# A spectral mixer with two expert layers on one core: new planner offsets, input in quarters, last spreads, gates and stores rearranged

## The chip, the core and the metric

The kernel runs on one core of a Trainium2 chip. The core has TensorE (PE in the rows; PEld is its weight load), VectorE (DVE), ScalarE (ACT), GpSimd (POOL) and SyncE (SP), each with its own instruction stream, and 16 DMA engines that serve the queues of SP, ACT and POOL. The metric is the device time of one execution in microseconds: 1768.54 us for the kernel before, the median of 3 runs (1767.31 to 1769.47).

## What is computed

The reference has three parts, each in float32, on 8 sequences of 3072 rows with 256 columns:

```
X = rfft(x, axis=1)                      # over the 3072 rows
Yr, Yi = complex product of X with (w_r, w_i), plus biases
y = irfft(soft_shrink(Yr) + i soft_shrink(Yi))

logits = y @ phi                         # 24576 rows, 8 experts x 4 slots
d = softmax over the rows;  slot_in = d.T @ y
slot_out = relu(slot_in @ w1) @ w2       # per expert, F = 1024
z = softmax over the slots of logits @ slot_out

out = (silu(z @ w_gate) * (z @ w_val)) @ w_out   # width 1536
```

The three moe2 weights come as float64, and the kernel makes float32 of them itself.

## The kernel before, in words

**First half (phase1, up to about 655 us).** The eight sequences are batches b = 0 to 7. Each goes through: stage_a (sixteen units; in each a matmul of 16 columns of x with a transform table into a PSUM bank, mm, and a transpose of that bank by VectorE into the tile chan, turn; there are two such banks), stage_c (the second step of the transform, in three blocks g = 0 to 2, with ScalarE, VectorE and GpSimd splitting its output in two parts), stage_b (the product with w_r and w_i, six products per block), after_b (bias and shrink, into the tile yt), stage_q (product with phi, and the transposes turn_y of yt), and the spreads: DMAs that carry yt to the tile yi with partitions and blocks exchanged, sixteen of 64 KB for each block. When the three blocks of a batch are done, logits, slots and combine follow. In logits, sp_out (L1031, ScalarE) fills one column of vpad, turn (L1017, VectorE) transposes vpad, and l_mm, colmax, keep_l, newmax, lower and expo come after one another. In slots, slot_mm (L1242) multiplies with the spread tile yi; its last two groups need the third block's. combine makes the scores over the slots and stores them to c_scr in DRAM. Beside these, narrow makes float32 of the float64 weights, and mix_w, part_w and rest_w prepare w_r and w_i once at the beginning.

**The order.** Every step is handed to a planner (class Plan) by add(engine, duration, rank, function, reads, writes, ...). The planner then emits the instructions one by one: among the tasks whose inputs are planned, it takes the one that can start first by its own times (COST and the durations given), and among those that can start together the one of lowest rank. A rank is a place in the batch sequence plus an offset from SHIFT, found by the task's name; a prime in the name is for the last batch, and a triple has one offset for each block. A name that is not in SHIFT has the offset 0. Engines execute in the order in which they were given their instructions. So SHIFT decides order and nothing else.

**The start.** load_f loads the table of stage_a, load_first (L681) the first batch in two halves of 128 columns, put the tables of stage_c (cm) and others, load_w (L1402) w_r, w_i and the biases by four DMAs; all are issued by SP.

**The end of the first half.** The third block of batch 7 is spread in four parts (yi_parts, L913) of four DMAs, all from SP. free_x, free_a and free_b close pools when their last readers are planned, and the expert weights (w1 and w2, sixteen loads of 1 MB by POOL's queue) go to the freed space. hold adds 80 small matmuls that write to a bank nobody reads.

**Second half (after_slots).** The 32 slots go through w1 and w2, then gates(t) (L1673) multiplies the result with a third of w_gate and w_val (t = 0, 1, 2, 512 columns each) and writes gstk. The main loop has 576 steps: gv(i) makes pg and pv of a block of 128 inner columns from gstk and the scores cst, split(i - 1) makes a high and a low part of silu(pg) * pv, and mm_out(i - 3) adds six products to the output banks; inner block f = i mod 12 needs the gate group t = f // 4. After each twelfth step two transposes and four DMAs store 512 rows' worth of output (L1732). The schedule of the loop is written out:

```
        for i in range(n + 3):
            for t in {0: (0, 1), 6: (2,)}.get(i, ()):
                gates(t)
            if i < n:
                gv(i)
            if 1 <= i <= n:
                split(i - 1)
            if i >= 3:
                mm_out(i - 3)
```

Of the kernel before, what the change touches and what calls it, by code (L numbers as in the profile page):

```python
# [10 lines left out]
F32 = mybir.dt.float32  # L11
# [11 lines left out]
R1 = 96  # L23
R2 = 32
# [135 lines left out]
for _n, _w in (  # L160
# [14 lines left out]


SHIFT = {
    "stage_a.mm": -9.84,
    "stage_a.turn": 0.54,
    "stage_c.mm": (-9.05, -7.24, -16.09),  # L180
    "stage_c.hi": (24.47, -33.15, -38.97),
    "stage_c.lo": (14.18, 18.71, -22.9),
    "stage_c.one_part": (-18.23, 22.67, -8.15),
    "stage_c.add_part": (-13.36, 13.63, -10.4),
    "stage_c.sum_hi": (14.45, 11.1, -10.23),
    "stage_c.sum_lo": (17.84, -9.25, -3.5),
    "stage_c.last_mm": (-1.22, 0.0, 0.0),
    "stage_c.last_out": (2.01, 0.0, 0.0),
    "stage_b.last_mm": (-3.14, 0.0, 0.0),
    "stage_b.last_out": (-37.61, 0.0, 0.0),  # L190
    "stage_b.mm": (-0.54, -0.28, -0.45),
    "after_b.take": (43.36, -0.88, 16.29),
    "after_b.gather": (-2.04, -56.11, 7.1),
    "after_b.relu": (29.62, 5.9, 11.56),
    "after_b.join": (8.77, 14.98, -9.65),
    "stage_q.mm": (0.04, -3.83, 3.24),
    "stage_q.turn_y": (-1.8, 21.9, 7.71),
    "stage_q.turn": (-17.81, 21.29, -10.62),
    "stage_q.spread": (9.56, -31.65, 30.86),
    "logits.inv_mm": -0.29,  # L200
    "logits.sp_mm": -20.44,
    "logits.sp_out": 3.1,
    "logits.rot": 25.23,
    "logits.join": -8.39,
    "logits.turn": -19.78,
    "logits.l_mm": 20.77,
    "logits.colmax": -10.52,
    "logits.keep_l": 6.71,
    "logits.spread": -20.81,
    "logits.max_mm": -6.92,  # L210
    "logits.newmax": 40.03,
    "logits.factor": 6.44,
    "logits.bc_mm": -20.03,
    "logits.lower": -9.17,
    "logits.expo": -9.83,
    "slots.f_mm": -1.07,
    "slots.turn": 7.27,
    "slots.cross": -13.47,
    "slots.rot": 1.28,
    "slots.join": -7.11,  # L220
    "slots.d_mm": -3.64,
    "slots.evac": -12.82,
    "slots.slot_mm": -9.92,
    "slots.gather": -15.51,
    "combine.rowmax": 14.19,
    "combine.lower": -34.43,
    "combine.expo": -29.05,
    "combine.total": 8.18,
    "combine.scale": -28.91,
    "combine.turn": -24.49,  # L230
    "combine.hi": 6.73,
    "combine.lo": 11.01,
    "combine.store": -13.51,
    "narrow.load": 18.5,
    "narrow.bits": -4.56,
    "narrow.size": 21.96,
    "narrow.value": -10.54,
    "narrow.store": 8.48,
    "load_x": 17.41,
    "narrow.part": 15.19,  # L240
    "narrow.rest": -35.44,
    "stage_q.mm'": (0.0, 0.0, -24.61),
    "stage_q.turn_y'": (0.0, 0.0, 7.19),
    "stage_q.turn'": (0.0, 0.0, 4.21),
    "stage_q.spread'": (0.0, 0.0, -25.35),
    "logits.inv_mm'": -24.89,
    "logits.sp_mm'": -13.07,
    "logits.sp_out'": 30.05,
    "logits.rot'": 3.97,
    "logits.join'": 15.9,  # L250
    "logits.turn'": -2.34,
    "logits.l_mm'": -42.59,
    "logits.colmax'": 37.25,
    "logits.keep_l'": 19.77,
    "logits.spread'": 15.02,
    "logits.max_mm'": -13.41,
    "logits.newmax'": -7.99,
    "logits.factor'": 24.36,
    "logits.bc_mm'": 12.34,
    "logits.lower'": -12.24,  # L260
    "logits.expo'": 34.68,
    "slots.f_mm'": 31.04,
    "slots.turn'": 17.34,
    "slots.cross'": 4.58,
    "slots.rot'": 0.07,
    "slots.join'": 40.67,
    "slots.d_mm'": 14.24,
    "slots.evac'": -15.02,
    "slots.slot_mm'": -41.69,
    "slots.gather'": -2.53,  # L270
    "combine.rowmax'": 29.49,
    "combine.lower'": -3.91,
    "combine.expo'": 1.28,
    "combine.total'": 25.68,
    "combine.scale'": 43.19,
    "combine.turn'": 51.36,
    "combine.hi'": -1.63,
    "combine.lo'": 2.88,
    "combine.store'": 10.46,
    "fetch_w1": -9.92,  # L280
    "fetch_w2": 8.18,
    "fetch_wg": 4.29,
}


# [208 lines left out]
def kernel(  # L494
# [79 lines left out]
    def phase1():  # L574
# [103 lines left out]
        add("DVE", 3.0, -9, setup_small, w=["small", "vpad", "M"])  # L678


        def load_first(dh):  # L681
            def go():
                T["x0", dh] = t = early.tile([R1, R2, 128], F32, name=f"x0{dh}")
                nc.sync.dma_start(
                    out=t, in_=x[0, :, dh * 128:(dh + 1) * 128].rearrange("(p n) d -> p n d", n=R2)
                )

            return go
# [15 lines left out]
        def stage_a(b, p, rank):  # L704
            dq, dd = divmod(p, 4)
            dh, d0 = dq // 2, (dq % 2) * 64 + dd * 16
            kq = ("xq", b, dq) if b else ("x0", dh)
            kt, ka = ("tt", b, dh), ("ac", "a", b, p)
            d1 = dd * 16 if b else d0

            def mm():
                pt = bank(ka, [128, R2, 16], "ac")
                nc.tensor.matmul(  # L713
                    out=pt, lhsT=fwd[:, 8 - 8 * dh:136 - 8 * dh], rhs=T[kq][:, :, d1:d1 + 16], start=True, stop=True
                )

            def turn():
                nc.vector.transpose(  # L718
                    out=chan[:, 12 * dh:12 * dh + 16, d0:d0 + 16, :].rearrange("p j d i -> p d j i"),
                    in_=T[ka].rearrange("p n d -> p d n"),  # L720
                )
# [192 lines left out]
            return [[e] for e in range(4)] if (b, g) == (B - 1, 2) else [list(range(4))]  # L914

        def yi_keys(b, g):
            return [("yi", b, g, part[0]) for part in yi_parts(b, g)]

        def stage_q(b, g, rank):

# [24 lines left out]

                return go

            def spread(part):
                def go():
                    if part[0] == 0:  # L950
                        sb(ypool, ki, [128, 2, 4, 2, 4, 32], "yi", 4)
                    for e in part:
                        for q in range(4):
                            nc.sync.dma_start(
                                out=T[ki][32 * q:32 * q + 32, :, e].rearrange("p h c s k -> p h (c s k)"),
                                in_=T[ky][32 * e:32 * e + 32, :, q].rearrange("p h c f -> p h (c f)"),
                            )
# [7 lines left out]
            add("DVE", 0.33, rank, turn, r=[(*kp, 0)], w=[(*kq, g)], new=("qt", kq) if g == 0 else None)  # L965
            for part in yi_parts(b, g):
                add(
                    "SP", 0.25 * len(part), rank, spread(part), r=[(*ky, eh, co) for eh in range(2) for co in range(2)],
                    w=[(*ki, part[0])], new=("yi", ki) if part[0] == 0 else None, bus=0.74 * len(part), dmas=4 * len(part),
                )  # L970

        def times(eng, out, v, tw):
            e = nc.vector if eng == "DVE" else nc.gpsimd
# [457 lines left out]
        for b in range(B):  # L1431
            t0 = 3 * b
            a0, a1 = t0 - 1.6, t0 - 0.45
            da = (a1 - a0) / 16
            for dh in range(2 * (b == 0)):
                add("SP", 0.06, -9 + dh, load_first(dh), w=[("x0", dh)], bus=4.37)
            for dq in range(4):
                if b == 0 and dq == 3:
                    constants(0)
# [95 lines left out]
        for t in (0, 1):  # L1535
            add(
                "SP", 0.12, TT + 0.9, fetch_wg(t), w=[("wg", t)], bus=2.91, dmas=2, new=("yt", ("wg", t)),
                after=[("ws", i) for i, (_, d) in enumerate(jobs) if len(d) == 1] + [("yi", last, 2, 0), ("w2", E - 2), "w2x"],
            )
        def hold(i):  # L1540

# [17 lines left out]
    def after_slots(ypool):  # L1559
# [150 lines left out]
        def mm_out(i):  # L1710
# [12 lines left out]
            if f == NF - 1:  # L1723

                for k in range(2):
                    nc.vector.transpose(
                        out=ob_t[0][:, :, k, :], in_=po_t[0][k].rearrange("p (n l) -> p n l", l=32)
                    )
                r0 = b * SEQ + q * 1024
                to = out[r0:r0 + 1024].rearrange("(l n) (c e) -> c l n e", n=32, c=4)  # L1730
                for c in range(4):
                    nc.sync.dma_start(  # L1732
                        out=to[c, :, 16 * rh:16 * rh + 16],
                        in_=ob_t[0][32 * c:32 * c + 32].rearrange("p n h o -> p n (h o)"),
                    )

        n = len(steps)
        for i in range(n + 3):
            for t in {0: (0, 1), 6: (2,)}.get(i, ()):
                gates(t)  # L1740
            if i < n:
                gv(i)
# [41 lines left out]
```

## Time and profile before

| | us |
|---|---|
| median of 3 runs | 1768.54 (1767.31 to 1769.47) |
| the profiled execution | 1769.84 |
| its span, first to last instruction | 1768.0 |
| TensorE busy in the span | 1704.9 |
| VectorE, ScalarE, GpSimd busy | 1276.0, 981.8, 307.8 |
| SP's DMA queue | 103.59 MB, 29.1% of the 16 DMA engines' time |
| POOL's DMA queue | 29.36 MB, 6.9% |

A row of a timeline has the start in us from the span's first instruction, the duration, the engine (SPq: the queue that SP issues to; the duration is that of the issuing), the line, the operation, the tiles written and read, how many instructions were merged into the row, and in brackets the idle time before it with what ended that. A matmul on float32 data is two records.

### The profile page before, as it was taken

How to read it: one execution, taken by the hardware profiler on the slowest of the kernel's cores; microseconds unless marked ns; L12 is line 12 of the kernel's file. 1: busy time of each engine (PE TensorE's matmuls, PEld its weight loads, DVE VectorE, ACT ScalarE, POOL GpSimd, SP SyncE). 2: the span in 40 equal slices, each digit the busy share in tenths (PEclk: the TensorE clock that was granted, in tenths of full speed). 3: DMA queues.
4: the chain of work that ended last, by engine and by line, in shares of the span. 5: the costliest groups of instructions: out<-in, count | busy, mean ns of one | idle time of the engine just before them, and what ended most of it. 6: DMA issues, size and time to landing. Idle time of an engine off the chain costs nothing.

```text
span 1768.0 us, 23212 instructions
## 1 busy us (share of the span) xinstructions
PE 1704.9 (96%) x8266; PEld 1292.7 (73%) x8266; DVE 1276.0 (72%) x2116; ACT 981.8 (56%) x1809; POOL 307.8 (17%) x292
## 2 busy tenths in 40 slices
PE   6999999999998989999999999999999999999998
PEld 3666565666665665888888888888888888888886
DVE  4678878787786544777777777777777777777776
ACT  1565545546563514556655566556665566655664
POOL 1335345445454641000000000000000000000000
PEclk9999999999999989999999999999999999999999
DMA  9456564564774497112112112113112113111111
GB/s 183 72 120 126 132 139 88 132 134 100 146 159 143 147 326 149 24 25 51 25 24 52 24 25 51 25 24 51 24 25 51 25 24 52 24 25 24 24 23 26
DMA packets 252292, 134.44 MB, mean 76 GB/s; under 512 B 196912, under 2 KB 237584, under 8 KB 252176
## 3 DMA queue, kind: packets, MB, share of 16 engines
q1 hardware_dynamic: 241968, 103.59, 29.1%
q0 software_dynamic: 10208, 29.36, 6.9%
q8 instruction: 65, 1.06, 0.3%
q14 instruction: 51, 0.42, 0.1%
HBM read 69.99 MB, written 37.75 MB: 61 GB/s over the span
## 4 chain that ended last, share of the span: by engine, by line
PE 89%; DVE 5%; ACT 2%; DMA 1%; issue 1%; SPq 1%; POOL 0%; DVEq 0%; ACTq 0%; POOLq 0%
PE o L1719 45%; PE pb L830 9%; PE pg L1694 8%; PE pv L1695 8%; PE ac L713 6%; PE ac L735 4%; PE ch L928 1%; PE pb L1545 1%; PE ch L1242 1%; PE ch L1054 1%; PE ch L1190 1%; PE ch L988 1%; PE ch L1146 1%; PE pg L1678 1%; SPq L673 0%
## 5 line engine op out<-in xcount | busy, mean ns | idle before, releaser
L1719 PE MATMUL o<-hh,wo 128*128 128x512 f32 x2304 | 723.0, 395 | 0.0
L1699 DVE TENSOR_TENSOR h<-sg,pv 128x512 f32<-128x512 f32 x576 | 394.4, 685 | 271.5 <-ACT sg L1697 270.1
L1697 ACT ACTIVATE sg<-pg 128x512 f32<-128x512 f32 x576 | 344.4, 598 | 421.7 <-PE pg L1694 421.7
L1719 PEld LDWEIGHTS o<-hh,wo 128*128 128x128 f32 x2304 | 434.6, 189 | 100.4
L1719 PE MATMUL o<-hl,wo 128*128 128x512 f32 x1152 | 454.1, 394 | 0.0
L1707 DVE TENSOR_TENSOR hl<-h,hh 128x512 fp32r<-128x512 f32 x576 | 393.6, 683 | 0.2
L1706 ACT ACTIVATE hh<-h 128x512 fp32r<-128x512 f32 x576 | 359.6, 624 | 0.7 <-DVE h L1699 0.7
L1719 PEld LDWEIGHTS o<-hl,wo 128*128 128x128 f32 x1152 | 216.4, 188 | 51.6 <-DVE hl L1707 0.2
L1694 PE MATMUL pg<-cst,gstk 96*128 96x512 f32 x576 | 228.2, 396 | 0.0
L1695 PE MATMUL pv<-cst,gstk 96*128 96x512 f32 x576 | 226.4, 393 | 0.7 <-DVE gstk L1681 0.7
L902 POOL TENSOR_TENSOR yt<-r,yt 128x512 f32<-128x512 f32 x95 | 124.9, 1315 | 223.8 <-ACT yt L893 124.5
L830 PE MATMUL pb<-xg,wh 128*128 128x512 f32 x384 | 146.9, 462 | 10.9 <-ACT yt L883 5.1
L1646 POOL DMA_DIRECT2D cst<-c_scr x24 | 13.5, 566 | 818.9 <-PE pv L1695 797.9
L1695 PEld LDWEIGHTS pv<-cst,gstk 96*128 96x128 f32 x576 | 110.0, 191 | 27.1 <-DVE gstk L1681 1.6
L1694 PEld LDWEIGHTS pg<-cst,gstk 96*128 96x128 f32 x576 | 108.2, 188 | 24.4 <-issue 0.5
L718 DVE STREAM_TRANSPOSE chan<-ac 128x512 f32<-128x512 f32 x128 | 88.1, 702 | 38.1 <-PE ac L713 35.3
L713 PE MATMUL ac<-xq,fwd 96*128 96x512 f32 x224 | 111.3, 607 | 3.7 <-DVE chan L718 1.7
L735 PEld LDWEIGHTS ac<-cm,chan 128*128 128x128 f32 x768 | 100.3, 199 | 17.0 <-issue 7.3
L830 PEld LDWEIGHTS pb<-xg,wh 128*128 128x128 f32 x384 | 67.5, 191 | 55.0 <-issue 23.0
L735 PE MATMUL ac<-cm,chan 128*128 128x128 f32 x768 | 104.5, 286 | 0.0
L757 DVE TENSOR_TENSOR xg<-ac,xg 128x512 fp32r<-128x512 f32 x96 | 65.4, 683 | 27.4 <-ACT sf L760 15.2
L776 POOL TENSOR_TENSOR sg<-sf,sg 128x256 fp32r<-128x256 f32 x95 | 71.0, 757 | 64.3 <-ACT sg L772 54.4
(147 smaller groups left out, 1583.8 us busy)
## 6 DMA issues: line engine op xcount, KB each, us to landing
yi<-yt SPq DMA_DIRECT2D x384, 64.0 KB, 2.1
out_dram<-ob SPq DMA_DIRECT2D x192, 128.0 KB, 2.8
xq<-in_x_dram SPq DMA_DIRECT2D x28, 768.0 KB, 7.2
cst<-c_scr POOLq DMA_DIRECT2D x24, 384.0 KB, 5.9
w1s<-in_moe_w_dram POOLq DMA_DIRECT2D x8, 1024.0 KB, 9.4
w2s<-in_moe_w_dram POOLq DMA_DIRECT2D x8, 1024.0 KB, 22.0
x<-in_x_dram SPq DMA_DIRECT2D x2, 1536.0 KB, 15.1
cvi<-in_moe_w_gate_dram SPq DMA_DIRECT2D x6, 512.0 KB, 6.4
```

The costliest lines, as they stand in the source:

```text
L713: nc.tensor.matmul(out=pt, lhsT=fwd[:, 8 - 8 * dh:136 - 8 * dh], rhs=T[kq][:, :, d1:d1 + 16], start=True, stop=True)
L718: nc.vector.transpose(out=chan[:, 12 * dh:12 * dh + 16, d0:d0 + 16, :].rearrange("p j d i -> p d j i"), in_=T[ka].rearrange("p n d -> p d n"),
L735: nc.tensor.matmul(out=pt[:, :, q:q + 2, i // 2, :], lhsT=chan[:, 16 * dh + j // 2, :, j % 2], rhs=cm[:, j, :].rearrange("p (c h k) -> p c ...
L830: nc.tensor.matmul(out=pt, lhsT=w[:, dh, m, es], rhs=xx, start=m != 1 and dh == 0 and n == 0, stop=dh == 1 and n == 2, skip_group_check=True,)
L902: e.tensor_sub(out=part(), in0=quarters(T[kr]), in1=part())
L1694: nc.tensor.matmul(out=pg, lhsT=gstk[:, 0, f * 128:(f + 1) * 128], rhs=rhs, start=True, stop=True)
L1695: nc.tensor.matmul(out=pv, lhsT=gstk[:, 1, f * 128:(f + 1) * 128], rhs=rhs, start=True, stop=True)
L1697: nc.scalar.activation(out=sg, in_=pg, func=AF.Silu)
L1699: nc.vector.tensor_mul(out=h, in0=sg, in1=pv)
L1706: nc.scalar.activation(out=hh, in_=h, func=AF.Copy)
L1707: nc.vector.tensor_sub(out=hl, in0=h, in1=hh.bitcast(F32))
L1719: nc.tensor.matmul(out=po_t[0][k], lhsT=w[:, f % 4, k * 128:(k + 1) * 128], rhs=a, start=(f == 0 and m == 0), stop=(f == NF - 1 and m == 2 ...
```

## The change

SHIFT: every entry of the table has a new value, and thirteen names are new in it (load_f, setup_small, load_first, put, free_early, load_w, mix_w, part_w, rest_w, free_x, free_a, free_b, hold). COST and the durations stay. load_first loads four quarters of 64 columns. In the third block of the last batch, each of the four parts is spread by two tasks: queries q = 0, 1 from SP and q = 2, 3 from ACT, which gives ACT eight DMA issues; wherever yi of that block is read or awaited, all eight keys stand. Of the last four stores, two go out from ACT. gates(1) moves from ahead of step 0 to ahead of step 2.

```diff
 SHIFT = {
-    "stage_a.mm": -9.84,
-    "stage_a.turn": 0.54,
...
+    "load_f": 2.81,
+    "setup_small": -9.39,
+    "load_first": -3.7,
+    "stage_a.mm": -28.93,
+    "stage_a.turn": 2.94,
+    "put": -0.33,
+    "free_early": -16.09,
+    "load_w": -25.29,
+    "mix_w": 3.51,
+    "part_w": -17.96,
...
-    "stage_q.spread'": (0.0, 0.0, -25.35),
+    "stage_q.spread'": (0.0, 0.0, -21.67),
...
-        def load_first(dh):
+        def load_first(dq):
             def go():
-                T["x0", dh] = t = early.tile([R1, R2, 128], F32, name=f"x0{dh}")
+                T["x0", dq] = t = early.tile([R1, R2, 64], F32, name=f"x0{dq}")
                 nc.sync.dma_start(
-                    out=t, in_=x[0, :, dh * 128:(dh + 1) * 128].rearrange("(p n) d -> p n d", n=R2)
+                    out=t, in_=x[0, :, dq * 64:(dq + 1) * 64].rearrange("(p n) d -> p n d", n=R2)
                 )
...
-            kq = ("xq", b, dq) if b else ("x0", dh)
+            kq = ("xq", b, dq) if b else ("x0", dq)
...
-            def spread(part):
+            def spread(part, dma=nc.sync, qs=range(4)):
                 def go():
-                    if part[0] == 0:
+                    if part[0] == qs[0] == 0:
                         sb(ypool, ki, [128, 2, 4, 2, 4, 32], "yi", 4)
                     for e in part:
-                        for q in range(4):
-                            nc.sync.dma_start(
+                        for q in qs:
+                            dma.dma_start(
...
+                if len(part) == 4:
+                    add("SP", 1.0, rank, spread(part), r=ys, w=[(*ki, 0)], new=("yi", ki), bus=2.96, dmas=16)
+                    continue
+
+                for dma, eng, qs in ((nc.sync, "SP", (0, 1)), (nc.scalar, "ACT", (2, 3))):
+                    add(
+                        eng, 1.2, rank, spread(part, dma, qs), r=ys, w=[(*ki, part[0], qs[0])],
+                        new=("yi", ki) if part[0] == qs[0] == 0 else None, bus=0.37, dmas=1,
+                    )
...
-            for dh in range(2 * (b == 0)):
-                add("SP", 0.06, -9 + dh, load_first(dh), w=[("x0", dh)], bus=4.37)
+            for dq in range(4 * (b == 0)):
+                add("SP", 0.06, -9 + dq / 4, load_first(dq), w=[("x0", dq)], bus=4.37)
...
-                    nc.sync.dma_start(
+                    (nc.scalar if i == n - 1 and c % 2 else nc.sync).dma_start(
...
-            for t in {0: (0, 1), 6: (2,)}.get(i, ()):
+            for t in {0: (0,), 2: (1,), 6: (2,)}.get(i, ()):
                 gates(t)
```

## Rows read from the trace of the kernel before

**Rows 1.** Stretches of the first half: stretch, length, engines' busy time (x), clock, DMA share, GB/s.

```profile
40.00:600.00 560.00, 530.35 (x2986) 361.50 (x2986) 430.26 (x748) 307.45 (x604) 253.69 (x227) 0.99 0.55 119
560.00:580.00 20.00, 14.86 (x48) 9.34 (x47) 11.85 (x25) 8.94 (x18) 5.91 (x6) 0.74 0.48 129
```

**Rows 2.** The same view, two stretches of stage_a of batch 0.

```profile
12.70:17.50 4.80, 4.75 (x6) 1.99 (x7) 1.44 (x2) 0.00 (x0) 0.00 (x0) 1.00 1.19 189
...
27.80:34.60 6.80, 6.80 (x9) 2.72 (x9) 3.01 (x5) 0.00 (x0) 2.12 (x2) 0.50 1.39 167
```

**Rows 3.** Timeline of the start: TensorE's stage_a, first and last weight issue of SP.

```profile
12.76 11.86 PE L713 MATMUL ac<-x,fwd 96*128 96x512 f32 x20 [12.76 <-DMA x<-in_x_dram]
15.24 0.43 SPq L1405 DMA_DIRECT2D wst<-in_w_r_dram  x1
...
17.72 1.04 SPq L673 DMA_DIRECT2D cm<-in_cmix_dram  x2
...
26.06 8.91 PE L713 MATMUL ac<-x,fwd 96*128 96x512 f32 x12 [1.45 <-DVE chan L718]
```

**Rows 4.** Input loads by line, with issue to landing: both halves, then two later quarters.

```profile
L684 SPq DMA_DIRECT2D x<-in_x_dram x2: 725/2540/4355, 1.2 to 2.0; - x2
...
DMA to landing us min/median/max: 11.4/15.1/18.7
...
L698 SPq DMA_DIRECT2D xq<-in_x_dram x2: 569/3221/5873, 22.6 to 23.4; - x2
...
DMA to landing us min/median/max: 10.4/12.2/14.0
```

**Rows 5.** Timeline at the end of the first half, some rows of SP, DVE, ACT, PE.

```profile
610.13 14.74 SPq L954 DMA_DIRECT2D yi<-yt  x16
625.59 0.37 SPq L1493 DMA_DIRECT2D fold<-in_csmall_dram  x1
626.85 19.41 SPq L954 DMA_DIRECT2D yi<-yt  x16
...
622.40 1.21 DVE L944 STREAM_TRANSPOSE yt<-yt 128x1024 f32<-128x1024 f32 x1
626.70 0.70 DVE L1017 STREAM_TRANSPOSE vt<-vpad 128x512 f32<-128x512 f32 x1
...
625.81 0.22 ACT L1031 ACTIVATE vpad<-ch 64x32 f32<-64x32 f32 x1 [6.25 <-PE ch L1026]
...
645.89 0.66 PE L1242 MATMUL ch<-yi,p 128*32 128x256 f32 x8 [0.58 <-ACT p L1207]
655.33 1.93 PE L1242 MATMUL ch<-yi,p 128*32 128x256 f32 x16 [7.42 <-DMA c_scr<-td]
```

**Rows 6.** Spreads of the last batch's second block, then third: issue to landing.

```profile
DMA to landing us min/median/max: 6.3/9.1/9.9
...
DMA to landing us min/median/max: 9.2/9.7/10.6
```

**Rows 7.** DMA queues from 628 to 644: packets, MB, share of 16 engines.

```profile
q0 software_dynamic: 1099, 4.24, 83.0%
q1 hardware_dynamic: 1094, 0.84, 21.0%
```

**Rows 8.** The view of rows 1, the stretch around the last slot matmuls.

```profile
652.00:662.50 10.50, 6.58 (x38) 2.83 (x42) 1.03 (x4) 0.00 (x0) 0.00 (x0) 0.52 0.96 356
```

**Rows 9.** TensorE's timeline from the gates to the first output matmul.

```profile
679.65 7.13 PE L1678 MATMUL pg<-wg,tail 128*128 128x512 f32 x16 [0.52 <-DVE tail L1664]
...
688.18 0.50 PE L1695 MATMUL pv<-cst,gstk 96*128 96x512 f32 x1 [0.69 <-DVE gstk L1681]
...
689.86 0.64 PE L1719 MATMUL o<-hh,wo 128*128 128x512 f32 x2
```

**Rows 10.** The last four stores: their issue, and issue to landing.

```profile
1762.49 2.19 SPq L1732 DMA_DIRECT2D out_dram<-ob  x4
...
DMA to landing us min/median/max: 2.2/2.8/3.0
```

More of the change, by code (lines that the diff above doesn't have):

```diff
@@ L177 @@
 SHIFT = {
-    "stage_a.mm": -9.84,
-    "stage_a.turn": 0.54,
[L180 to L244, printed above, removed]
-    "stage_q.spread'": (0.0, 0.0, -25.35),
[L246 to L282, printed above, removed]
+    "load_f": 2.81,
[8 more added lines that the diff above has]
+    "part_w": -17.96,
+    "rest_w": -0.28,
@@ new lines @@
+    "stage_c.mm": (-12.22, -1.28, -5.52),
+    "stage_c.hi": (53.77, -42.32, -55.05),
+    "stage_c.lo": (40.1, 19.86, -25.02),
+    "stage_c.one_part": (2.25, -2.27, 4.93),
+    "stage_c.add_part": (-68.16, 19.01, -25.95),
+    "stage_c.sum_hi": (10.97, 9.66, -13.31),
+    "stage_c.sum_lo": (-6.92, -75.37, -42.83),
+    "stage_c.last_mm": (36.23, 0.0, 0.0),
+    "stage_c.last_out": (-24.98, 0.0, 0.0),
+    "stage_b.last_mm": (-10.11, 0.0, 0.0),
+    "stage_b.last_out": (3.76, 0.0, 0.0),
+    "stage_b.mm": (-0.22, -0.26, -0.14),
@@ new lines @@
+    "after_b.take": (48.09, 1.97, 4.29),
+    "after_b.gather": (-37.89, -92.44, -12.86),
+    "after_b.relu": (21.51, 7.9, 2.96),
+    "after_b.join": (-54.79, -9.98, 9.41),
+    "stage_q.mm": (0.0, -9.39, 7.88),
+    "stage_q.turn_y": (7.74, 49.03, -2.46),
+    "stage_q.turn": (-12.53, -0.89, 4.91),
+    "stage_q.spread": (-23.98, -39.91, 59.31),
+    "logits.inv_mm": -18.3,
+    "logits.sp_mm": -38.62,
+    "logits.sp_out": 26.62,
+    "logits.rot": 64.93,
+    "logits.join": -32.12,
+    "logits.turn": -71.72,
@@ new lines @@
+    "logits.l_mm": 44.13,
+    "logits.colmax": -29.68,
+    "logits.keep_l": 51.42,
+    "logits.spread": 15.76,
+    "logits.max_mm": 33.28,
+    "logits.newmax": 26.07,
+    "logits.factor": 18.59,
+    "logits.bc_mm": -2.58,
+    "logits.lower": -7.03,
+    "logits.expo": -25.93,
+    "slots.f_mm": -12.38,
+    "slots.turn": 9.73,
+    "slots.cross": -27.68,
+    "slots.rot": -4.89,
+    "slots.join": -8.33,
+    "slots.d_mm": -36.49,
+    "slots.evac": -14.41,
+    "slots.slot_mm": -32.07,
@@ new lines @@
+    "slots.gather": -18.97,
+    "combine.rowmax": 14.04,
+    "combine.lower": 1.85,
+    "combine.expo": -54.13,
+    "combine.total": -16.96,
+    "combine.scale": -4.82,
+    "combine.turn": -12.43,
+    "combine.hi": -27.19,
+    "combine.lo": 7.86,
+    "combine.store": -22.54,
+    "narrow.load": 28.3,
+    "narrow.bits": 1.55,
+    "narrow.size": 21.04,
+    "narrow.value": -7.49,
+    "narrow.store": -31.84,
+    "load_x": 0.13,
+    "narrow.part": 9.87,
+    "narrow.rest": 4.99,
+    "stage_q.mm'": (0.0, 0.0, -7.18),
@@ new lines @@
+    "stage_q.turn_y'": (0.0, 0.0, 12.3),
+    "stage_q.turn'": (0.0, 0.0, 20.63),
+    "stage_q.spread'": (0.0, 0.0, -21.67),
+    "logits.inv_mm'": -32.46,
+    "logits.sp_mm'": -32.14,
+    "logits.sp_out'": 25.91,
+    "logits.rot'": 31.71,
+    "logits.join'": -6.39,
+    "logits.turn'": -6.55,
+    "logits.l_mm'": -67.64,
+    "logits.colmax'": 60.65,
+    "logits.keep_l'": 33.35,
+    "logits.spread'": 13.57,
+    "logits.max_mm'": -18.0,
+    "logits.newmax'": 9.47,
+    "logits.factor'": 18.28,
@@ new lines @@
+    "logits.bc_mm'": 12.87,
+    "logits.lower'": -25.45,
+    "logits.expo'": 35.72,
+    "slots.f_mm'": 59.73,
+    "slots.turn'": 49.73,
+    "slots.cross'": 30.87,
+    "slots.rot'": -12.01,
+    "slots.join'": 52.75,
+    "slots.d_mm'": 12.44,
+    "slots.evac'": -2.82,
+    "slots.slot_mm'": -78.14,
+    "slots.gather'": -22.49,
+    "combine.rowmax'": 5.14,
+    "combine.lower'": -35.75,
+    "combine.expo'": -34.15,
+    "combine.total'": 20.3,
+    "combine.scale'": 53.34,
+    "combine.turn'": 70.78,
@@ L283 @@
+    "combine.hi'": 5.94,
+    "combine.lo'": -32.53,
+    "combine.store'": 28.18,
+    "free_x": -27.72,
+    "free_a": 45.67,
+    "free_b": 2.84,
+    "fetch_w1": 13.94,
+    "fetch_w2": -26.03,
+    "fetch_wg": -14.12,
+    "hold": 25.89,
 }
@@ L706, in stage_a @@
             dh, d0 = dq // 2, (dq % 2) * 64 + dd * 16
-            kq = ("xq", b, dq) if b else ("x0", dh)
+            kq = ("xq", b, dq) if b else ("x0", dq)
             kt, ka = ("tt", b, dh), ("ac", "a", b, p)
-            d1 = dd * 16 if b else d0
+            d1 = dd * 16
             def mm():
@@ L916, in yi_keys @@
         def yi_keys(b, g):
-            return [("yi", b, g, part[0]) for part in yi_parts(b, g)]
+            return [("yi", b, g, p[0], *h) for p in yi_parts(b, g) for h in ([()] if len(p) == 4 else [(0,), (2,)])]
         def stage_q(b, g, rank):
@@ L965, in stage_q @@
             add("DVE", 0.33, rank, turn, r=[(*kp, 0)], w=[(*kq, g)], new=("qt", kq) if g == 0 else None)
+            ys = [(*ky, eh, co) for eh in range(2) for co in range(2)]
             for part in yi_parts(b, g):
[L967 to L970, printed above, removed]
+                if len(part) == 4:
[6 more added lines that the diff above has]
+                    )
         def times(eng, out, v, tw):
@@ L1537, in phase1 @@
                 "SP", 0.12, TT + 0.9, fetch_wg(t), w=[("wg", t)], bus=2.91, dmas=2, new=("yt", ("wg", t)),
-                after=[("ws", i) for i, (_, d) in enumerate(jobs) if len(d) == 1] + [("yi", last, 2, 0), ("w2", E - 2), "w2x"],
+                after=[("ws", i) for i, (_, d) in enumerate(jobs) if len(d) == 1] + yi_keys(last, 2) + [("w2", E - 2), "w2x"],
             )
```

## The prediction

> **What bounds the kernel now.** I read the busy time in stretches first, then the order of instructions at the start and at the end of the first half, the issue-to-landing times of the transfers there, and last the packets of each DMA queue. From 40 to 600 us TensorE is busy 530.35 of 560 us [rows 1]: the first half is bound by TensorE, with 29.65 us of idle time spread over it, of which 5.14 lie in the one stretch 560 to 580. The second half runs from about 690 us to the end, and the change does not touch its steps. So time can come from four places: the start (TensorE's first matmul is at 12.76 us, and from 27.8 to 34.6 its granted clock is 0.50, that is 1.2 of 2.4 GHz) [rows 2, 3]; the idle time between 40 and 600; the last batch's slot matmuls, of which the last sixteen wait 7.42 us until 655.33 [rows 5], after which the granted clock is 0.52 up to 662.5 [rows 8]; and the last stores.
>
> The profiled execution took 1769.84 us, its span 1768.0 and 1.84 around it. That is 1.30 above the median of the runs, 1768.54. The terms are added to 1769.84, and 1.30 is taken off at the end.
>
> **Start.** Rank decides among transfers that could all be issued at time zero. By the new offsets load_w has -2.0 - 25.29 = -27.3, load_f -17.2, the four quarters -12.7 to -11.9, the first table -8.2. So the four weight transfers, which stood behind that table, now go first. They held SP's queue from 15.24 to 17.72 [rows 3], 2.48 us; the first quarter is issued at 3.7, the first half was at 1.2. The halves landed 11.4 and 18.7 us after issue, at 12.6 and 20.7: one half is 8.05 us of stream behind 3.4 us of start-up [rows 4]. Two later transfers of just a quarter's shape, issued at 22.6 and 23.4, landed at 33.0 and 37.4, 4.4 us apart [rows 4]. So the quarters land at 3.7 + 3.4 + 4.4 = 11.5, then 15.9, 20.3 and 24.8. The first matmul comes 1.1 us sooner, the last input 4.1 us later.
>
> What counts is when the sixteen units of stage_a (two matmuls each) are done, now at 26.06 + 8.91 = 34.97 [rows 3]. The first run at half pace, 6 matmuls in 4.8 us [rows 2]; in the middle TensorE stands 1.45 us, because mix_w holds VectorE ahead of a transpose, and then runs 6.8 us at 1.2 GHz [rows 2, 3]. In the new order the weights land near 6 us, so mix_w fits into VectorE's idle time ahead of the first matmul. From 11.5: 4.8 us at half pace give 2.8 units; the other 13.2, at the 0.97 us that two PSUM banks and one 0.7 us transpose per unit allow, take 12.8 us: 29.1. The last quarter allows 24.8 + 4 x 0.97 = 28.7. That is -5.9 if the clock holds. If it falls for as long as now, half of 6.8 us goes: -2.5. I take -4.5, between the two. The ends are -6, and 0 where the last four units run at half pace (31.7) and the stage behind them too (3.4 more). TensorE-bound work follows, so the term stands to the end. The first table and the tables behind it land 2 to 4 us later; stage_c needs them after 29 only, so that is hidden, at up to 2 us if stage_a is faster than I think.
>
> **New order in the middle.** Offsets only choose among instructions that could start together, and the cost tables stay: no work is added or removed, and what changes is which of the 29.65 us of waits remain. The trace cannot show the new order. Bounds: nine tenths of that idle time gone (-27), or twice as much (+30). The nearest row is the worst stretch: 560 to 580 has 5.14 us of idle time, and its granted clock of 0.74 costs about another 4 [rows 1]. An order without such a place gains 9 us, one that keeps it nothing. I take half, -4.5.
>
> **Last spreads.** The second block of batch 7 is spread by sixteen 64 KB transfers issued from 610.13 on, the third by sixteen from 626.85 to 646.26 [rows 5]. These leave 1.21 us apart and land 9.7 us after issue [rows 5, 6]: 9.7 / 1.21 = 8, so SP keeps eight under way, and each further one waits until the one eight before it has landed. Between 628 and 644 the queue of the expert weights put through 1099 packets and SP's 1094 [rows 7]: the engines serve one packet of each in turn, whatever its size. A spread is 64 pieces of 1 KB on 16 engines, four each and a closing one; by the shares a turn takes 0.193 + 0.049 us, five turns 1.21, just the issue distance. With a third queue at work a turn takes 0.29 us and moves two spreads in 1.46 us, so spreads on ACT's queue would go nearly twice as fast. The block is transposed at 623.6 [rows 5].
>
> The Trainium skill (DMA: Bandwidth & Descriptors, Issuing engines are not separate DMA queues) says that issuing from several engines saves only the sequencer's issue time. By that rule the last spread lands when it does now and this part gives nothing. The Trainium skill (same page, Queues, rings and completion order) also has an engine take its queues in turn by packets; the count above agrees with that sentence.
>
> The price is on ACT. Its eight issues stand in order ahead of sp_out, which ran at 625.81 and for which VectorE's transpose at 626.70 waits [rows 5]; behind that transpose hangs the chain to the slot matmuls at 645.89. If the limit of eight counts both queues together, ACT's first issue waits for the twelfth of the second block's spreads: the first landed at 616.4, the sixteenth at 634.1 [rows 6], so about 630. Pairs alternate between the queues, and ACT's last issue waits for an ACT spread that itself could leave only when the fold table, issued at 625.59, had landed (636): about 639. ACT is free at 639.6, the transpose runs 12.9 us later than now, and the slot matmuls start at 658.8. The last spreads are there by then (about 646), so they take 2.0 + 1.0 us and end at 661.8 instead of 657.26: +4.5. If ACT's queue has its own allowance, ACT loses 8 x 0.62 = 5.0 us from 623.6 (the weights' issue distance [rows 3]), the chain is 2.1 us late (648.0), and SP's half lands at 634.1 + 2.0 (turns shared) + 2.0 (fold) + 8 x 1.21 = 647.8: end at 651.0, -6.3, and without the long wait the 4.6 us up to 662.5 at half pace save 2.3 [rows 8]: -8.6. No row shows which holds. I take the first, +4.5, since eight under way is all that the rows show; the ends are -10 and +9 (the clock lower on the chain too).
>
> **Gates and stores.** Now both gate groups run together from 679.65 to 686.78, the bank of the last one is free 1.40 us later, at 688.18, and the first output matmul is at 689.86 [rows 9]. With one group alone, pv waits out those 1.4 us less one matmul of 0.24; after the second group a wait of 0.69 comes again as now. +0.9 with a wait for hl at the output gone; ends -0.5 and +1.4. The four last stores are issued over 2.19 us and land 2.2 to 3.0 us after issue, the last at 1766.95 [rows 10]. Two queues issue the last one about 0.9 us sooner, and nothing stands behind them: -0.9, ends -1.3 and 0.
>
> Sum: 1769.84 - 4.5 - 4.5 + 4.5 + 0.9 - 0.9 = 1765.3; less 1.30, **1764.0 us** (A).
>
> **Rivals.** B: ACT's spreads are not held, -8.6 for +4.5: 1750.9. For it: ACT's queue is empty until then. Against: SP is held at eight throughout. C: both queues share today's pace and the chain stays inside it, 0 for +4.5: 1759.5; the count of packets speaks against it. The first sentence cited from the Trainium skill (DMA: Bandwidth & Descriptors, Issuing engines are not separate DMA queues) speaks for it. D, the slower side: the new order opens one more place like 560 to 580, +9 for -4.5, with ACT held as in A: 1777.5. It is slower than before by more than can be told once the middle loses 3.6 us. For it: the order of some 2986 matmuls is new and the plan knows neither the clock nor the limit of eight. Against: the offsets move no work.
>
> **How the numbers follow.** A 0.50, B 0.24, C 0.08, D 0.18. A alone spans 1755 to 1773. The range 1748 to 1777 leaves out the lower third of B and half of D. A change under 0.2%, 3.5 us, cannot be told from none by this kernel's runs. Faster (below 1765.0): 0.55 of A, B, nearly all of C: 0.58. Slower (above 1772.1): most of D and a tenth of A: 0.21. The same: 0.21.
>
> **What would show it.** Start: weights first on SP, first matmul near 11.5, stage_a done near 30, and whether the clock falls near 27. Middle: TensorE's idle time from 40 to 600, about 25 us. End: ACT's issues waiting for landings, sp_out some 14 us after the block's transpose, no wait of TensorE for spreads. If ACT issues its eight in 5 us, B is right; if the last spread still lands 31 us after the transpose, C. Output less than 10.2 us after the first gate matmul would refute +0.9. I am wrong in kind if the middle moves by more than 10 us.

## The result, and the profile after

The changed kernel takes 1748.2 us (median of 4 runs, 1746.4 to 1749.42) where the kernel before takes 1767.97 beside it: a ratio of 0.9889, 95% interval 0.9876 to 0.9901. The forecast was 1764.0, the range 1748 to 1777. The median lies inside that range by 0.2 us, and this is luck: the range reaches so low for rival B, which did not come, and theory A by itself spanned 1755 to 1773. The direction is right, and so are the sizes of the start, the last spreads and the gates; the middle gained four times what was forecast for it, and by the prediction's own last sentence that is wrong in kind.

The profiled execution has a span of 1747.6 us where 1768.0 stood, 20.4 less. Cut at points that both kernels have, the difference is:

| stretch | before, us | after, us | difference | forecast |
|---|---|---|---|---|
| to the end of stage_a of batch 0 | 34.97 | 29.52 | -5.45 | -4.5 |
| from there to sp_out of batch 7 (the middle) | 590.84 | 572.78 | -18.06 | -4.5 |
| from there to the last slot matmul's end | 31.45 | 35.67 | +4.22 | +4.5 |
| from there to the first gate matmul | 22.39 | 20.27 | -2.12 | 0 |
| from there to the first output matmul | 10.21 | 11.25 | +1.04 | +0.9 |
| from there to the last output matmul's end | 1071.85 | 1071.77 | -0.08 | 0 |
| last stores, issue to last landing | 4.46 | 4.53 | +0.07 | -0.9 |

**The middle.** Stretches of the kernel after: the first two answer to [rows 1], the third is the middle as cut above, the last three are its batches 1 to 4, 5 and 6, and 7, each from the first layer matmul of a batch on. Columns as there: length, then busy time of TensorE, its weight loads, VectorE, ScalarE and GpSimd (instructions), granted clock, DMA share, GB/s.

```profile
40.00:600.00 560.00, 543.79 (x3109) 371.33 (x3108) 443.92 (x755) 314.54 (x615) 269.57 (x243) 0.99 0.60 134
560.00:580.00 20.00, 14.94 (x74) 10.40 (x73) 16.69 (x22) 10.70 (x23) 17.42 (x17) 0.94 0.61 202
29.52:602.30 572.78, 555.91 (x3185) 382.51 (x3184) 450.71 (x772) 320.53 (x631) 274.76 (x249) 0.99 0.62 136
93.74:382.10 288.36, 284.39 (x1631) 192.11 (x1629) 238.64 (x412) 161.46 (x320) 133.15 (x117) 1.00 0.60 126
382.10:526.70 144.60, 139.89 (x796) 93.81 (x796) 122.87 (x207) 83.18 (x161) 71.97 (x66) 1.00 0.61 130
526.70:602.30 75.60, 68.48 (x439) 51.09 (x438) 50.76 (x85) 39.54 (x78) 45.76 (x44) 0.95 0.68 213
```

The same stretches of the kernel before, by its own times:

```profile
34.97:625.81 590.84, 558.64 (x3189) 383.86 (x3187) 443.94 (x774) 321.26 (x630) 273.03 (x246) 0.99 0.57 128
100.40:404.70 304.30, 287.31 (x1639) 194.35 (x1638) 241.69 (x413) 163.32 (x320) 134.46 (x117) 1.00 0.58 124
404.70:543.60 138.90, 136.16 (x732) 92.63 (x732) 114.69 (x206) 82.82 (x165) 72.81 (x67) 1.00 0.62 136
543.60:625.80 82.20, 73.07 (x499) 53.17 (x497) 48.95 (x87) 39.48 (x73) 42.36 (x40) 0.94 0.52 162
```

Read the length against the first number behind it. In the middle TensorE works 558.64 us before and 555.91 after, but the idle time falls from 32.20 to 16.87 us. Most of that is in batches 1 to 4: 304.30 us become 288.36, and 17.0 us idle become 4.0. Batches 5 and 6 take 5.7 us longer and batch 7 6.6 less (796 matmuls where 732 stood, and 439 for 499: work moved from one to the other). The stretch 560 to 580, on which the forecast hung, has as much idle time as before (5.06 us, 5.14 in [rows 1]), but in other work. Before, TensorE waited there for VectorE's transposes of batch 6's logits (L1054, 1.42 and 2.15 us) and for an exponential (1.50 us):

```profile
565.26 1.99 PE L1054 MATMUL ch<-vt,csm 128*96 128x512 f32 x2 [2.15 <-DVE vt L1017]
```

In the kernel after, the same matmuls run without a wait, the logits' by 545. What is idle there is mostly a matmul of batch 6's slots (L1209), which waits 2.96 us until 579.08 for VectorE; the granted clock is 0.94 in this stretch and 0.89 in the next 20 us. So the place that the forecast meant is gone, and another of its size has opened. What the new order removed in the whole middle, the waits of TensorE say (who waited for whom, us in total, times, longest). Before, in the middle:

```profile
PE ch L1054 <- DVE vt L1017: 8.6, 7, 2.2
PE pb L830 <- ACT yt L883: 5.1, 7, 1.3
PE pb L830 <- DVE xg L757: 4.4, 4, 1.8
PE ch L988 <- DVE qt L939: 2.8, 3, 0.9
```

After:

```profile
PE ch L1209 <- DVE vpad L1198: 3.8, 3, 3.0
PE ac L726 <- DVE chan L731: 3.3, 11, 0.4
PE pb L843 <- ACT yt L896: 2.1, 3, 1.0
```

The logits' matmuls (L1054 before) waited seven times, 1.2 us in the mean, for VectorE's transpose, and the layers' matmuls (L830) eleven times in the two rows shown for their inputs. Of the first nothing is left in the list; of the second, with the rows not shown, 5.0 us of 11.4 (L843 after). The new order puts other matmuls into these places.

**The start.** Timeline of the kernel after, answering to [rows 3]: start, length, engine, line, operation.

```profile
0.74 0.44 SPq L1424 DMA_DIRECT2D wst<-in_w_r_dram  x1
3.27 13.11 SPq L697 DMA_DIRECT2D x<-in_x_dram  x4
10.82 18.70 PE L726 MATMUL ac<-x,fwd 96*128 96x512 f32 x32 [10.82 <-DMA x<-in_x_dram]
```

The weights go first, the quarters follow, and stage_a runs as one row of 32 matmuls from 10.82 to 29.52 without the break of [rows 3]. The half clock of [rows 2] is still there, but short: 3.41 us at 0.50, after stage_a.

```profile
34.78:38.19 3.41, 3.41 (x14) 3.12 (x15) 1.84 (x6) 1.42 (x4) 0.73 (x1) 0.50 1.39 170
```

**The last spreads.** The end of the first half in the kernel after, answering to [rows 5]:

```profile
602.30 0.22 ACT L1050 ACTIVATE vpad<-ch 64x32 f32<-64x32 f32 x1 [7.48 <-PE ch L1045]
602.36 17.76 ACTq L967 DMA_DIRECT2D yi<-yt  x8
605.23 14.93 SPq L967 DMA_DIRECT2D yi<-yt  x8
620.17 0.29 ACT L1122 ACTIVATE fac<-mst,mst 128x1 f32<-128x1 f32 x1 [17.65 <-DMA yi<-yt]
622.37 3.78 PE L1165 MATMUL ch<-td,csm 96*128 96x512 f32 x4 [8.93 <-ACT td L1147]
635.06 0.66 PE L1261 MATMUL ch<-yi,p 128*32 128x256 f32 x8 [0.58 <-ACT p L1226]
```

ACT has only eight transfers to issue and is held at them for 17.76 us; an allowance of eight of its own would have let them go in 8 x 0.62 = 5 us. What lets them go is SP's landings: ACT's second issue leaves at 606.41, when one spread of ACT's and six transfers of SP's are under way and a spread of SP's (issued at 597.87, 8.5 us to landing) has just landed. So the limit of eight under way counts both queues. ACT's next operation, at 620.17, comes 17.65 us after the one before, and TensorE waits 8.93 us behind it. During that wait the clock falls to 0.50:

```profile
618.46:628.70 10.24, 6.33 (x17) 4.26 (x18) 5.63 (x8) 3.55 (x6) 4.07 (x3) 0.50 0.87 270
637.97:658.24 20.27, 18.42 (x219) 8.68 (x219) 4.13 (x37) 4.13 (x6) 9.47 (x12) 1.00 1.04 268
```

The second row answers to [rows 8]: what follows the slots now runs at full clock. The kernel before had half clock for as long, 10.24 us, but from 652.26 to 662.50, across the end of the slots, so that what followed them ran at 0.88 in the mean:

```profile
657.26:679.65 22.39, 20.66 (x220) 9.53 (x219) 4.15 (x37) 4.13 (x6) 6.27 (x10) 0.88 0.76 194
```

That is the -2.12 of the table, which the forecast did not have.

**Stores.** The last four stores of the kernel after, answering to [rows 10]:

```profile
1742.04 0.85 SPq L1751 DMA_DIRECT2D out_dram<-ob  x2
1742.05 0.94 ACTq L1751 DMA_DIRECT2D out_dram<-ob  x2
```

The last issue ends at 1742.99, 0.95 us after the first begins, where one queue took 2.19; the last landing is at 1746.57, 4.53 us after the first issue, where it was 4.46.

### The profile page after: what moved, and what is told of

It reads as the page before. It is cut to its first block, busy times and chain, and to the rows that moved or that the text cites. A ratio compares the mean times of both kernels' runs of the same rounds, so it can differ in the third digit from the quotient of the medians.

```text
span 1747.6 us, 23245 instructions
## 1 busy us (share of the span) xinstructions
PE 1700.3 (97%) x8266; PEld 1291.0 (74%) x8266; DVE 1283.0 (73%) x2114; ACT 981.0 (56%) x1809; POOL 308.0 (18%) x294
## 4 chain that ended last, share of the span: by engine, by line
PE 85%; DVE 8%; DMA 3%; ACT 2%; issue 1%; SPq 1%; POOL 0%; DVEq 0%; ACTq 0%; POOLq 0%
PE o L1738 46%; PE pg L1713 8%; PE pv L1714 8%; PE pb L843 7%; PE ac L726 6%; PE ac L748 4%; PE ch L941 1%; DMA yi<-yt 1%; PE ch L1007 1%; PE ch L1209 1%; DVE yt L957 1%; DVE cv L1361 1%; DVE chan L731 1%; DVE xg L770 1%; DMA c_scr<-ls 1%
## 5 line engine op out<-in xcount | busy, mean ns | idle before, releaser
L843 PE MATMUL pb<-xg,wh 128*128 128x512 f32 x384 | 141.2, 449 | 3.3 <-ACT yt L896 2.1
L843 PEld LDWEIGHTS pb<-xg,wh 128*128 128x128 f32 x384 | 66.3, 190 | 41.9 <-issue 17.3
L767 ACT ACTIVATE xg<-ac 128x512 fp32r<-128x512 f32 x96 | 56.7, 595 | 48.1 <-PE ac L748 46.3
```

The costliest lines, as they stand in the source:

```text
L843: nc.tensor.matmul(out=pt, lhsT=w[:, dh, m, es], rhs=xx, start=m != 1 and dh == 0 and n == 0, stop=dh == 1 and n == 2, skip_group_check=True,)
```

## The experiments

Theories at the start: (T1) the new offsets' order gives the gain, the split of the spreads costs because ACT is held, gates cost 1 us, stores give nothing; (T2) the gain in the middle comes from the feed (weights first, quarters), or the split is what pays. Unless said otherwise, a run changes the kernel after, and "before" beside it is 1767 to 1768 us.

**e1: the new offsets alone, in the kernel before.**

```
 SHIFT = {
-    (offsets of before)
+    (offsets of after)
 }
```

> The kernel before with nothing changed but the offsets of the first half's planner. If the new order is the main gain (my theory after the result), the stretch from the end of the first projection to the first half's last output multiply shrinks by 15 to 18 us and the kernel takes 1750 to 1755 us, without a gain at the start and with the last spreads from SP alone as before. If the gain of the middle comes from the start (weights first, input in quarters), the middle keeps its 590 us and the time is 1766 to 1769 us. If the split of the last spreads were what pays (the rival), the time is above 1760 us.

Measured: 1747.97 us (1747.4 to 1748.82), ratio 0.9891 [0.9876, 0.9906]. The whole gain of the change is in the offsets; all its other parts together come to nothing (their sum is taken apart below). The middle is 575.87 us, 15.0 less than before, and its batches 1 to 4 are those of the kernel after:

```profile
100.70:389.10 288.40, 284.35 (x1631) 192.14 (x1630) 238.59 (x412) 161.53 (x320) 133.09 (x117) 1.00 0.61 126
```

The time is 2 us better than expected at its best: stage_a of batch 0 is done at 32.53 (2.4 sooner, where no gain was expected: the offsets put the weights first, mix_w no longer stands in the middle of stage_a, and the clock does not fall there), the slots end 29.01 us after sp_out (2.4 sooner, with SP's queue alone), and the 2.1 us of clock behind the slots come too.

**e2: the old offsets in the kernel after.**

```
 SHIFT = {
-    (offsets of after)
+    (offsets of before)
 }
```

> The kernel after with the offsets of before; all the rest of the change stays. If the order is the main gain: the start gives -5.5 us, the spreads cost +4.2, the gates +1.0, the stores 0, so 1767.5 to 1769.5 us, no gain over before. If the rest of the change carries the gain: 1750 to 1757 us.

Measured: 1770.68 us (1769.75 to 1772.12), ratio 1.0018 [1.0009, 1.0028]. The rest of the change without the offsets is slightly slower. Its quarters, here ahead of the weights, end stage_a at 26.03, 8.94 us sooner, and the rest loses that again: 3.1 in the middle, 8.0 at the spreads (ACT held in the same way), 1.0 at the gates, against 2.1 gained behind the slots. The first half of T2 falls as far as the quarters go; weights first is itself one of the offsets, and e12 takes it back.

**e3: the last spreads from SP alone.**

```
-                for dma, eng, qs in ((nc.sync, "SP", (0, 1)), (nc.scalar, "ACT", (2, 3))):
-                    add(
-                        eng, 1.2, rank, spread(part, dma, qs), ...
+                add(
+                    "SP", 0.25, rank, spread(part), ...
```

> The kernel after with the last batch's spreads all issued by SP, as before. If ACT's held queue is the price of the split, ACT's logits and the slot matmuls no longer wait for its last issue: the stretch from the last output multiply to the slot matmuls' end falls from 35.7 to 31 us and the time from 1748.2 to 1743 us (1741 to 1745). If the split pays (the rival): the wait for the last spread is back, 7.4 us, and the time is 1752 to 1756 us.

Measured: 1741.37 us (1740.3 to 1742.22), ratio 0.9853 [0.9838, 0.9869]: 6.9 us less than with the split. The end of the first half:

```profile
602.51 20.39 SPq L967 DMA_DIRECT2D yi<-yt  x16
611.06 1.08 ACT L1092 ACTIVATE ls<-ch 96x512 f32<-96x512 f32 x2 [9.37 <-DMA c_scr<-ls]
612.98 1.23 ACT L1146 ACTIVATE td<-td 96x512 f32<-96x512 f32 x2 [0.67 <-DVE td L1136]
615.31 3.00 PE L1164 MATMUL ch<-td,csm 96*128 96x512 f32 x4
627.95 0.66 PE L1260 MATMUL ch<-yi,p 128*32 128x256 f32 x8 [0.58 <-ACT p L1225]
628.48 2.37 PE L1260 MATMUL ch<-yi,p 128*32 128x256 f32 x40
```

ACT's exponential (td) runs at 612.98, 8.71 us sooner than with the split (621.69), and the slots end 29.38 us after sp_out instead of 35.67. TensorE does not wait for a spread either, though SP sends all sixteen: the 7.42 us wait of [rows 5] is gone without the split. It is gone less because the spreads are sooner than because the chain beside them is later. The last spread lands 26.9 us after sp_out (at 628.3), where it was 29.1 (654.9); the slot matmuls start 26.5 us after sp_out, where it was 20.1.

What makes the chain later is the first ACT row above. ACT's copy of the logits (ls) waits 9.37 us for a store of batch 6's ls to land, which SP issued at 600.23, behind the sixteen spreads of the second block; the kernel before had sent that store before these spreads, at 604.11, and did not wait. With the split the store lands at 612.4, while ACT is still held. So this store is the next wait at the end of the first half, and no run moves it.

**e4: the gate groups as before.**

```
-            for t in {0: (0,), 2: (1,), 6: (2,)}.get(i, ()):
+            for t in {0: (0, 1), 6: (2,)}.get(i, ()):
```

> The kernel after with the gate groups of before. If the later gate group costs what the trace shows (11.25 us from the first gate matmul to the first output matmul, where 10.21 stood before): 1.0 us faster, 1747.2 us. If that stretch differs for another reason: 1748.2 us within 0.5.

Measured: 1748.08 us (1744.48 to 1748.44): no verdict by the time, whose spread is wider than the 1 us in question. The trace decides it: from the first gate matmul to the first output matmul this run takes 10.21 us, as before the change, for 11.25.

```profile
658.25:668.46 10.21, 9.51 (x24) 4.42 (x25) 4.35 (x7) 4.54 (x10) 1.65 (x3) 1.00 1.76 319
```

**e5 and e6: new offsets for one group of tasks, old ones for the others.** In e5 the names stage_a, stage_b, stage_c, after_b and stage_q keep the new values, in e6 logits, slots and combine; loads, frees and fetches have the old ones in both.

```
 SHIFT = {
-    (all offsets of after)
+    (offsets of after for the group, of before for the rest)
 }
```

> The kernel after with the new offsets for the tasks of the projections and layers only (names stage_a, stage_b, stage_c, after_b, stage_q); logits, slots, combine, loads and fetches keep the old ones. All old was 1770.7 us, all new 1748.2. If the gain sits in the layers' order: 1750 to 1755 us. If it sits in where logits and slots stand between the layers (the old order's largest waits are logits' turns): 1763 us or more. If the fit works only as a whole: 1768 us or more, and the next run too.

> The kernel after with the new offsets for logits, slots and combine only; layers, loads and fetches keep the old ones. If the gain sits in where logits and slots stand: 1752 to 1757 us (most of the 22.5 us from 1770.7). If in the layers: 1765 us or more. If only the whole set fits: 1768 us or more.

Measured: e5 1784.12 us (1783.03 to 1786.07), e6 1800.28 (1799.14 to 1801.78). Both are slower than all old and all new, by 13 and 30 us over all old. The question "which group carries the gain" has no answer: neither group does by itself. The offsets of loads, frees and fetches alone were not run.

**e7: ACT's half of the spreads behind its last exponential.**

```
-                        eng, 1.2, rank, spread(part, dma, qs), r=ys, w=[(*ki, part[0], qs[0])], ...
+                        "ACT", 1.2, rank, spread(part, nc.scalar, (2, 3)), ...
+                        dmas=1, after=[("td", "d", b, 0), ("td", "d", b, 1)],
```

> The kernel after with ACT's half of the last spreads put behind ACT's last exponential of the logits, so that nothing of the logits stands behind a held issue; the split over two queues stays. If the price of the split is ACT held at its issues: 1740 to 1744 us, as with all spreads on SP (1741.4). If the price is the two queues' transfers themselves (or the hold merely moves to the slots' evictions): 1746 to 1750 us.

Measured: 1742.33 us (1741.83 to 1743.76), ratio 0.9859 [0.9844, 0.9873].

```profile
614.37 1.23 ACT L1154 ACTIVATE td<-td 96x512 f32<-96x512 f32 x2 [0.66 <-DVE td L1144]
615.69 6.39 ACTq L969 DMA_DIRECT2D yi<-yt  x6
```

ACT's exponential now runs at 614.37, ahead of the issues, of which six still take 6.39 us. With the split kept and only its place on ACT moved, 5.9 of the 6.9 us come back. So the price was what stood behind ACT's held issues, not the two queues' transfers.

**e8: spreads from SP, gates as before, stores from SP** (the edits of e3 and e4, and the line below).

```
-                        (nc.scalar if i == n - 1 and c % 2 else nc.sync).dma_start(
+                        nc.sync.dma_start(
```

> The kernel after with three parts undone: last spreads from SP alone, gate groups as before, last stores from SP alone. If the three prices add (-6.9, -1.0, 0): 1740.4 us, between 1739.5 and 1741.5. If two store queues do help by the time of their issues: 1741.3 us or more.

Measured: 1739.16 us (1738.49 to 1741.46), ratio 0.9842 [0.9825, 0.9858]: the fastest of this study, 9 us under the changed kernel with three of its parts taken out. The four last stores take 4.43 us from issue to last landing (4.53 with two queues). The median lies 0.3 us under the interval expected. Its profiled run shows why a run can do better than the sum: TensorE's clock was not lowered near 34 and 577 us, as it was in e3, whose program is the same up to the gates. sp_out came 3.9 us sooner, of which 1.7 are left at the end of the slots (629.15 for 630.85), since ACT waits longer for the store (11.6 us for 9.4). First e3, then e8, whose work runs 1.5 to 3.9 us sooner in this stretch:

```profile
570.00:590.00 20.00, 15.44 (x111) 10.53 (x112) 12.38 (x15) 7.15 (x12) 13.54 (x13) 0.83 0.89 315
```

```profile
570.00:590.00 20.00, 15.96 (x139) 11.19 (x139) 12.48 (x14) 8.54 (x13) 13.60 (x12) 1.00 0.95 346
```

The idle time there is the same (4.6 and 4.0 us); the clock fell in one and not in the other. So a microsecond or two between e3 and e8 is not the edits'.

**e9 and e10: how exact the offsets must be.** e9 takes the mean of the old and the new offsets, e10 rounds the new ones to multiples of 2 us.

```
 SHIFT = {
-    "stage_a.mm": -28.93, ...
+    "stage_a.mm": -19.385, ...      (e9)
+    "stage_a.mm": -28.0, ...        (e10)
```

> The kernel after with each offset half way between the old value (nothing where there was none) and the new one. If the gain grows with the offsets, as a distance gone towards a better place: 1757 to 1762 us, half way between all old (1770.7) and all new (1748.2). If each set is good only as a whole, as the two mixed sets suggest (1784.1 and 1800.3): 1775 us or more.

> The kernel after with every new offset rounded to the nearest multiple of 2 us, so that none is off by more than 1 us. If the gain needs only the coarse places: 1746 to 1752 us. If it is a fit to one exact order: 1755 us or more, a third or more of the 22.5 us between all new and all old given back.

Measured: e9 1794.43 us (1793.91 to 1797.39), e10 1773.93 (1769.31 to 1776.31). Half way between the two sets lies a worse one than either, and moving every offset by at most 1 us gives back the whole gain and 3 us more (25.7 in all). Batches 1 to 4 of e10:

```profile
90.60:399.00 308.40, 292.02 (x1629) 199.45 (x1628) 243.79 (x416) 161.64 (x318) 129.78 (x113) 0.98 0.62 126
```

308.40 us for 288.36, with 16.4 us idle again for 4.0, and 7.6 us more of busy time at a clock of 0.98. The kernel before had as much idle time in these batches (17.0 us) at a clock of 1.00, so the amount of idle time alone does not tell the clock.

**e11 and e12: the start, on e8.** e11 loads the first input in halves again; e12 takes one offset back, that of load_w, so that the weights come behind the quarters.

```
-                add("SP", 0.06, -9 + dq / 4, load_first(dq), w=[("x0", dq)], bus=4.37)
+                add("SP", 0.06, -9 + dh, load_first(dh), w=[("x0", dh)], bus=4.37)
```

```
-    "load_w": -25.29,
```

> The kernel of run e8 (1739.2 us) with the first input in halves again. By the start alone (first projection done at 32.5 us with halves and new offsets, 28.5 to 29.5 with quarters) it is 3.0 us slower: 1742.2. If the order that follows from the halves differs enough, the middle moves too and the time is 1745 us or more; if quarters bring nothing: 1739.2 within 1.5.

> The kernel of run e8 with one offset taken back, that of the mixing weights' loads, so that they come behind the input's quarters again. By the start alone (first projection done at 26.0 us in e2, which loads in that order, 29.0 in e3): 3 us faster, 1736. If the weights then come late for the first mixing, or one offset out of the set spoils the order as the mixed sets did: 1741 us or more.

Measured: e11 1748.11 us (1746.99 to 1749.36), e12 1743.8 (1742.11 to 1745.63). The quarters are worth 9 us against e8's median, of which 3.7 are the sooner end of stage_a (32.15 for 28.49); the rest of batch 0 gives most of the others. (sp_out comes 10.7 us later in e11's trace than in e8's, and 2.3 of them are won back behind it, where ACT waits 10.3 us for the store and not 11.6.) Below, from the end of stage_a to the first layer matmul of batch 1, e3, e11 and e12 (e3 and not e8, for the clock's sake):

```profile
28.95:93.00 64.05, 62.98 (x324) 45.41 (x324) 38.44 (x69) 36.21 (x75) 23.76 (x25) 0.97 0.61 104
```

```profile
32.15:100.50 68.35, 63.81 (x323) 45.26 (x324) 39.01 (x69) 36.38 (x75) 24.14 (x25) 0.98 0.50 85
```

```profile
26.31:95.90 69.59, 65.21 (x326) 47.20 (x325) 40.60 (x74) 37.65 (x78) 27.47 (x28) 0.95 0.61 107
```

With halves, 4.5 us are idle there for 1.1, in waits for layer inputs. With the weights behind, stage_a ends 2.6 us sooner than in e3, but TensorE then waits for the mixed weights (1.5 us at wh, 0.6 at wl) and its clock is lower, 0.95: the stretch is 5.5 us longer, and batch 1 starts 2.9 us later. Both differ from e3 only up to batch 1: the steady order of the batches behind it is the same. Both times lie where they were expected if more than the start changed.

## Why the prediction was right or wrong

- **Start, -4.5: right** (-5.45). e1 splits it: 2.4 by the new offsets alone, with the break and the half clock gone from stage_a though its first matmul is 1.6 us later (14.32 for 12.76), and 3.0 by the quarters. Weights first is not needed for a sooner end: in e12, with the weights behind, stage_a ends 2.6 us sooner than in e3, and the price comes at the mixed weights. The prediction left out that the quarters go on paying in batch 0 after stage_a.
- **New order in the middle, -4.5: this is the term that failed**, -18.06 measured. "The nearest row is the worst stretch ... An order without such a place gains 9 us, one that keeps it nothing. I take half." The new order took that place away and opened another of its size (5.06 us idle in the same stretch; in small, that is what rival D said). The gain came from elsewhere: the small waits of 1 to 2 us that recur in the batches are gone, 13.0 us of idle time in four batches. The price should have come from the steady batches' idle time (17.0 of 304.30 us) and not from one stretch; the idle total of 29.65 us was in [rows 1]. The term's bound of -27 held it, but the range did not go by that bound; the sign was not to be had from the trace before. "Offsets move no work", said against rival D, is true and beside the point: e5, e6, e9 and e10 move no work either and are 6 to 33 us slower than before.
- **Last spreads, +4.5: the number right, the mechanism half.** The limit of eight that counts both queues is shown (A, and not B). But the prediction held sp_out behind ACT's issues. With both orders sp_out goes ahead of them (602.30 and 602.36; in e2 619.93 and 632.35), and it is fac and the exponential, in e2 the exponential, that are held (620.17, 641.81). And the price is larger than the table's: without the split the new order would have had 29.4 us here, so the split costs 6.3 in the trace and 6.9 in the median, and 8.0 in the old order (e2). So the agreement of +4.22 with +4.5 is luck in part.
- **Gates, +0.9: right** (+1.04; e4 takes it back in the trace). The waits are the forecast ones: pv waits 1.17 us after the first group (1.40 less 0.24 was forecast) and 0.72 after the second.
- **Stores, -0.9: wrong, 0.** The issues were shortened by 1.24 us, and the last landing did not move: 4.53 us after the first issue for 4.46, and 4.43 in e8. The Trainium skill (DMA: Bandwidth & Descriptors, Issuing engines are not separate DMA queues), cited for rival C, says that a second issuing engine saves issue time alone. The stores agree with it and more, since here even the saved issue time bought nothing. For the spreads it is closer to the trace than "nearly twice as fast" was: sixteen left over 17.2 us with two queues and over 19.8 with one (issues from 602.36 to 619.57, and 602.51 to 622.32), and the last landed at 627.1 for 628.3.
- **Left out:** 2.12 us of clock between the slots and the gates. The 10.24 us at half clock are as long as before and lie ahead of the last slot matmuls now, so this term and the +4.22 belong together.

Sum in the table's terms: -5.45 - 18.06 + 4.22 - 2.12 + 1.04 - 0.08 + 0.07 = -20.38, and -20.4 in the spans. Against e1, the parts other than offsets are: quarters 6.1 us less up to sp_out (608.40 to 602.30), split 6.7 more, gates 1.0 more: 1.6, as the spans differ (1746.0 and 1747.6).

## What to carry to other kernels

Price a reordering by the idle time of the loop's steady part, which an order can remove in every turn, and give it a wide range of both signs: a set of offsets is good only as a whole, and one rounded or mixed has to be measured as a new kernel. After a new order, take each of the other edits back once: a remedy (the split spreads) may answer a wait that the order has hidden behind another one, and keep its price. A transfer's issue belongs on an engine on which nothing urgent stands behind it, since it may be held until others land.

## What the runs showed of the hardware

Eight transfers under way is a limit over SP's and ACT's queues together: ACT was held 17.76 us for eight issues of its own, 9.41 us in e2, and did nothing else meanwhile. In e2 each of ACT's issues leaves within 0.1 us of a landing of SP's (the second at 633.59, the last at 641.17, landings at 633.6 and 641.1). And the clock is not a function of the program alone: with the same order and much the same idle time (4.6 and 4.0 of 20 us), one execution, e3's, ran at 0.83 and another, e8's, at 1.00, worth 3.9 us at sp_out and 1.7 at the end of the slots. These two ran on different chips; but e7's four executions, on one chip, differ in the same way (mean clock 0.994 with spans of 1742.0 and 1740.9 us, 0.997 with 1740.2 and 1740.1).
